# A second buffer for the exps computed on VectorE, one slot for Q's weights, and another plan of which exp blocks go there

## The chip, the cores and the metric

One NeuronCore of a Trainium2 chip runs the whole kernel. The metric is the device time of one execution in microseconds, as a median over runs.

## The reference

Two branches work on the same x (2048 tokens of 1024 features) and a sigmoid gate mixes them per token. A is a state-space model (SSM) with a complex diagonal recurrence, B is attention with 32 heads of 32 features.

```python
g = sigmoid((x * gate_w).sum(-1, keepdims=True))
# A
Lam_bar = exp(exp(log_dt) * Lam);  B_bar = ((Lam_bar - 1) / Lam)[:, None] * Bmat
h_t = Lam_bar * h_(t-1) + B_bar x_t            # complex, 1024 states
a = 2 * (h @ Cmat.T).real + x * Dskip
# B
q, k, v = split_heads(x @ wqkv)                # 32 heads of 32
b = softmax(q k^T * 32 ** -0.5) v  @ wo
out = g * a + (1 - g) * b
```

## The kernel before

**The loop.** Attention sets the order. It goes through 8 groups of 4 heads; a group has 8 units of 256 queries, and a unit 8 bursts of 256 keys. That makes 512 bursts, numbered 0 to 511; unit U holds bursts 8U to 8U+7. `burst` writes 8 score matmuls (L1615) to two of three PSUM slots and two exps of 128x1024 on ScalarE (L1634), one for each pair of heads. `pv` multiplies the results with V (L1700) some bursts later, and `normalize` (L1713, L1714) closes a unit.

**Exps shared with VectorE.** `X_PLAN` and `X_AT` choose bursts in pairs. In a chosen burst the second exp covers only 768 of its 1024 columns (L1631). For the other 256, VectorE reads the scores into a fixed-point tile `xi` (L1624, "the read"). The short exp on ScalarE also waits for this read, since its operation has it in `deps`. When both bursts of a pair have been read, `x_ops` gives three polynomial steps on VectorE (L1658, L1659, L1655) and one on GpSimd (L1656); `x_pv` then multiplies the result with V (L1679). `xi` holds one pair. So, ahead of a chosen burst, `build` runs whatever steps are still pending:

```python
            while p in self.x_of and self.xbg:
                self.x_flush()
            second = self.burst(p)
```

`X_AT` is ((0, 2), (4, 6)): an entry of `X_PLAN` that is a multiple of 8 takes bursts 0 and 2 of its unit, the other kind bursts 4 and 6. There are 92 entries, from 112 to 504, so 184 short exps.

**Everything else** is cut into dense chains of 8 or more matmuls, of which some four go into each burst: the projections to Q, K (`d_qk`, L1418) and V (`d_v`, L1436), the SSM's input chains u (`d_u`, L1448), its output chains c (`d_c`, L1495, L1501) and the output projection (`d_out`, L1526). Each chain ends in an evacuation of PSUM bank 7 on VectorE: L1425, L1442, L1452 (u), L1508 (c), L1538. Between those, VectorE does the work of the SSM: tables (L1328, L1331), folding factors into C (`fold_ops`, L1311 to L1313), and for each of 32 items (8 blocks of states by 4 stretches of time) elementwise steps (L1346) and scans (L1355).

**The planner.** `build` writes the order out when the program is made. It keeps a guess of VectorE's time (`dve_t`) with a cost for each step, and puts as many waiting steps into each burst as end in time for the next evacuation. Output chains of a stretch of time begin once its items are done and all of C is folded.

**Weights.** `wb` has two slots of Q, K and V weights (one for even groups, one for odd) and three of B. `ld_w` loads all three parts for the group after next at burst 25 of a group. Wo's rows later take the place of weights that have had their last use: `wo3` and `wo` name the places. All these DMAs are issued by SyncE (SP), whose queue runs in order.

Of the kernel before, what the change touches and what calls it, by code (L numbers as in the profile page):

```python
# [922 lines left out]
GROUPS = 8  # L923
QUNITS = 8
BURSTS = 8
NBURST = GROUPS * QUNITS * BURSTS
# [7 lines left out]

X_AT = ((0, 2), (4, 6))
X_PLAN = (112, 116, 120, 124, 128, 132, 136, 140, 144, 148, 152, 156, 160, 164, 168, 172, 176, 180, 184, 188, 192, 196, 200, 204, 208, 212, 216, 220, 224, 228, 232, 236, 240, 244, 248, 252, 256, 260, 264, 268, 272, 276, 280, 284, 288, 292, 296, 300, 304, 308, 312, 316, 328, 352, 356, 360, 364, 368, 372, 376, 380, 384, 388, 392, 396, 400, 404, 408, 412, 416, 420, 424, 428, 432, 436, 440, 444, 448, 452, 456, 460, 464, 468, 472, 476, 480, 484, 488, 492, 496, 500, 504)
X_COLS = 256
# [5 lines left out]
X_A = SCALE * math.log2(math.e) * 65536.0  # L943
X_LO = -127.0 * 65536.0
# [14 lines left out]
class FastPath:  # L959

    def __init__(self, nc, S, es, d, flag):
        self.nc, self.S, self.d, self.flag = nc, S, d, flag
        E = es.enter_context
        T = lambda name, shape, dt: E(nc.sbuf_tensor("f_" + name, shape, dt))
# [20 lines left out]
        self.hp = hp  # L985
        self.hpx = wb[:, 6144:9216].rearrange("p (k n) -> p k n", k=6)
# [71 lines left out]
    def ld_x(self, i, eng="sp"):  # L1058

        for r, n in ((0, 128), (1, 128)) if i == 0 else ((2 * i, 256),):  # L1060
            self.dma(lambda e, r=r, n=n: e.dma_start_transpose(self.xT[:, :, 128 * r:128 * r + n], self.x2[128 * r:128 * r + n, :]),  # L1061
                     [], [("xr", r + k) for k in range(n // 128)], "ld_x", eng)

    def ld_w(self, g, part, eng="sp"):
        cb = 1024 * part + 128 * g
        self.dma(lambda e: e.dma_start(self.w[:, g % 2, part], self.wsrc[:, :, cb:cb + 128]), [], [("w", g % 2, part)], "ld_w", eng)

# [54 lines left out]
    def piece(self, part, i, bank, first):  # L1122

        ps, w, xT = self.ps, self.w, self.xT
        for h in range(2):
            r = 2 * i + h

            def mm(e, r=r, h=h):
                m = None
                for a in range(8):  # L1130
                    m = e.matmul(ps[:, bank, 128 * h:128 * (h + 1)], w[:, 0, part, a, :], xT[:, a, 128 * r:128 * (r + 1)], start=(a == 0), stop=(a == 7))
                return m
            kw = dict(writes=[("bank", bank)]) if h == 0 else dict(acc=[("bank", bank)])
            yield lambda mm=mm, kw=kw, r=r: self.S.op("pe", mm, reads=[("w", 0, part), ("xr", r)], name="proj", **kw)

    def half256(self, part, i, half):
        ps, w, xT = self.ps, self.w, self.xT

        def mm(e):
            m = None  # L1140
            for a in range(4 * half, 4 * half + 4):
                m = e.matmul(ps[:, 7, 0:256], w[:, 0, part, a, :], xT[:, a, 256 * i:256 * (i + 1)], start=(a == 0), stop=(a == 7))
            return m
        self.S.op("pe", mm, reads=[("w", 0, part), ("xr", 2 * i), ("xr", 2 * i + 1)], name="proj", **(dict(acc=[("bank", 7)]) if half else dict(writes=[("bank", 7)])))

    def opening(self):
        S, ps, w, xT, dve = self.S, self.ps, self.w, self.xT, self.dve

# [8 lines left out]
        for word in self.OPENING.split():  # L1157
            op = word.rstrip("0123456789.")
            i = word[len(op):]
# [16 lines left out]
            elif op in ("Va", "Vb"):  # L1176
                bank, h, kt = 6, int(op == "Vb"), 2 * i + int(op == "Vb")
# [236 lines left out]
    def d_qk(self, g, part, ch, bank=7):  # L1414
        ps, w, xT = self.ps, self.w, self.xT
        mms = []
        for a in range(8):
            mms.append((1, lambda e, f, l, a=a: e.matmul(ps[:, bank, :], w[:, g % 2, part, a, :], xT[:, a, 512 * ch:512 * (ch + 1)], start=f, stop=l),  # L1418
                        [("w", g % 2, part)] + self.xtok(ch)))
        if part == 0:  # L1420
            z = (4 * g + ch) % 5
            dst, tok = self.Q[:, z, :], ("Q", z)
        else:
            dst, tok = self.K[:, g % 2, 512 * ch:512 * (ch + 1)], ("K", g % 2, ch)
        return self.chain(mms, "proj", lambda: self.dve(lambda e: e.tensor_copy(dst, ps[:, bank, :]), [("bank", bank)], [tok], "evac_qk"), bank)  # L1425

    def d_v(self, g, f, bank=7):
        ps, w, xT = self.ps, self.w, self.xT
        mms = []
        for q in range(4):  # L1430
            kt = 4 * f + q
            for half in range(2):
                def fn(e, first, last, q=q, kt=kt, half=half):
                    m = None
                    for a in range(4 * half, 4 * half + 4):
                        m = e.matmul(ps[:, bank, 128 * q:128 * (q + 1)], xT[:, a, 128 * kt:128 * (kt + 1)], w[:, g % 2, 2, a, :],  # L1436
                                     start=(a == 0), stop=(a == 7))
                    return m
                mms.append((1, fn, [("w", g % 2, 2)] + self.xtok(f)))
# [163 lines left out]
    def burst(self, B):  # L1603
# [17 lines left out]
        if mine is not None:  # L1621
            b, n = mine
            s = sl[1]
            first = self.dve(lambda e: e.tensor_scalar(self.xi[:, X_COLS * n:X_COLS * (n + 1)], ps[:, 2 * s + 1, 512 - X_COLS:512], X_A, X_LO, ALU.mult, ALU.max),  # L1624
                             [("S", s)], [("xi", n)], "x_in")
        def exp(z):
# [17 lines left out]
    def x_ops(self, b):  # L1644

        xi, xq, xp = self.xi, self.xq, self.xp
# [4 lines left out]
        i2, p2 = [("xi", 0), ("xi", 1)], [("xp", 0), ("xp", 1)]  # L1651

# [72 lines left out]
    def build(self):  # L1725
# [55 lines left out]
        for p in range(first, NBURST):  # L1781
# [40 lines left out]
            if pg == 25 and g + 2 < GROUPS:  # L1822
                assert g or not (proj[0] or cur and cur.tag == "proj")
                for part in (1, 2, 0):
                    self.ld_w(g + 2, part)
            wsv = self.d["B_wo"].rearrange("(a p) n -> p a n", p=128)
            if p == 386:
                self.dma(lambda e: e.dma_start(self.wo3[0], wsv[:, 0:3, :]), [], ["wo0"] + [("w", 0, q) for q in range(3)], "ld_wo")
            if not cs and cur is None and not wo1 and self.c_left[3] == 0:
                wo1 = True  # L1830
                self.dma(lambda e: e.dma_start(self.wo3[1], wsv[:, 3:6, :]), [], ["wo1"] + [("bT", r) for r in range(3)] + [("hp", 8, k) for k in range(6)], "ld_wo")
            if g >= 6 and not wo6 and not cs and self.c_left[3] == 0:
                wo6 = True
                self.dma(lambda e: e.dma_start(self.wo3[3], wsv[:, 6:7, :]), [], ["wo3", ("cT", 0, 0), ("cTf", 0, 0, 0), ("cTf", 0, 0, 1)], "ld_wo")
            if g >= 6 and not last and not proj[7] and not us and not cs and cur is None and not self.bg:

                last = True
                xs = [("xr", r) for r in range(16)]
                assert wo1 and wo6
                self.dma(lambda e: e.dma_start(self.wo3[2], wsv[:, 7:8, :]), [], ["wo2"] + [("w", 1, q) for q in range(3)] + xs, "ld_wo")  # L1840
            if g >= 6 and not cs and self.c_left[3] == 0 and nal < 8 and p > self.c_end:
# [280 lines left out]
```

## Time and profile before

| | |
|---|---|
| median of 3 runs | 931.43 us (930.91 to 931.58) |
| profiled execution, its own time | 928.48 us |
| its span, first to last instruction | 926.7 us |
| mean granted TensorE clock | 0.998 |
| ScalarE busy | 908.3 us, 1034 instructions |
| TensorE busy | 883.7 us, 15095 matmuls |
| VectorE busy | 758.9 us, 1310 instructions |
| GpSimd busy | 74.4 us, 156 instructions |

In the profile's rows PE is TensorE, PEld its weight loads, ACT ScalarE, DVE VectorE, POOL GpSimd and SPq SyncE's issue of DMAs. A row of the groups has line, engine, operation, out<-in and shapes with their count, then total busy us and mean ns of one, then the engine's idle us just before them and who ended it. A row of the timeline has start and length in us; a bracket at its end is the idle time before it and its releaser. Consecutive alike instructions are merged into one row (x3).

### The profile page before, as it was taken

Reading aid. Unit: us, or ns where it says so; the run is one execution under the profiler, and the core shown is the slowest. Engines: PE = TensorE matmul, PEld = TensorE weight load, DVE = VectorE, ACT = ScalarE, POOL = GpSimd, SP = SyncE. Lnnn points to the kernel's source line nnn. Section 1 sums busy time; section 2 is a strip of 40 time slices with the busy share of each in tenths; the row PEclk is TensorE's granted clock in tenths of the full one; section 3 lists DMA queues with packets and bytes.
Section 4 is the critical chain, followed back from the end, with each engine's and each line's share of the span. In section 5 each row is a group of like instructions: output and inputs, shape, how many; then the busy total and the mean of one; then the engine's idle time right before and its main releaser. Section 6 shows DMA issues by size and latency. Waiting matters only on the chain.

```text
span 926.7 us, 33866 instructions
## 1 busy us (share of the span) xinstructions
PE 883.7 (95%) x15095; PEld 502.8 (54%) x15316; DVE 758.9 (82%) x1310; ACT 908.3 (98%) x1034; POOL 74.4 (8%) x156
## 2 busy tenths in 40 slices
PE   8899999999999999999999999999999999989995
PEld 4555744447555565556655565555655655545553
DVE  2789989888989989889898989998998655676665
ACT  6999999999999999999999999999999999999997
POOL 2000000000100100102110100100010010001000
PEclk9999999999999999999999999999999999999999
DMA  9579737730114305572011511523002012424312
GB/s 205 93 127 167 115 80 137 156 86 16 42 53 102 70 20 102 120 160 52 19 51 53 122 38 27 120 64 102 19 17 65 21 48 74 145 85 123 118 63 75
DMA packets 170920, 77.71 MB, mean 84 GB/s; under 512 B 147216, under 2 KB 155408, under 8 KB 170768
## 3 DMA queue, kind: packets, MB, share of 16 engines
q1 hardware_dynamic: 168608, 74.94, 35.9%
q8 instruction: 121, 1.98, 0.9%
q10 hardware_dynamic: 2160, 0.53, 0.3%
q14 instruction: 31, 0.25, 0.1%
HBM read 25.18 MB, written 20.97 MB: 50 GB/s over the span
## 4 chain that ended last, share of the span: by engine, by line
PE 51%; ACT 36%; DVE 8%; issue 2%; DMA 1%; SPq 1%; DVEq 0%; ACTq 0%
ACT f_pt L1634 28%; PE f_ps L1700 11%; PE f_ps L1615 11%; PE f_ps L1495 8%; PE f_ps L1418 8%; PE f_ps L1448 6%; PE f_ps L1436 5%; ACT f_pt L1631 4%; DVE f_xi L1624 3%; ACT f_cT L1634 2%; ACT f_OT L1634 1%; ACT f_Et L1634 1%; SPq L1061 1%; PE f_ps L1679 1%; DMA f_xT<-in_A_x_dram 1%
## 5 line engine op out<-in xcount | busy, mean ns | idle before, releaser
L1634 ACT ACTIVATE f_pt<-f_ps 128x1024 bf16<-128x1024 f32 x760 | 727.7, 1113 | 1.2 <-PE f_ps L1615 1.0
L1700 PEld LDWEIGHTS f_ps<-f_V,f_pt 128*128 128x128 bf16 x7184 | 222.4, 96 | 94.8 <-issue 67.5
L1700 PE MATMUL f_ps<-f_V,f_pt 128*128 128x33 bf16 x7184 | 257.9, 178 | 0.3 <-ACT f_pt L1634 0.3
L1615 PE MATMUL f_ps<-f_Q,f_K 32*128 32x256 bf16 x4096 | 203.4, 273 | 14.4 <-ACT f_pt L1634 5.6
L1631 ACT ACTIVATE f_pt<-f_ps 128x768 bf16<-128x768 f32 x184 | 162.8, 885 | 3.0 <-DVE f_xi L1624 1.6
L1615 PEld LDWEIGHTS f_ps<-f_Q,f_K 32*128 32x128 bf16 x4096 | 60.8, 92 | 152.3 <-ACT f_pt L1634 125.4
L1448 PE MATMUL f_ps<-f_xT,f_wb 128*128 128x512 bf16 x448 | 117.7, 379 | 7.9 <-issue 2.3
L1418 PE MATMUL f_ps<-f_xT,f_wb 128*128 128x512 bf16 x406 | 106.7, 379 | 4.2 <-DVE f_K L1425 0.3
L1656 POOL TENSOR_SCALAR f_xp<-f_xq 128x512 int16<-128x512 f32 x92 | 57.3, 623 | 603.5 <-DVE f_xq L1655 385.9
L1624 DVE TENSOR_SCALAR f_xi<-f_ps 128x256 int32<-128x256 f32 x184 | 77.7, 423 | 19.5 <-PE f_ps L1615 13.7
L1355 DVE TENSOR_TENSOR_SCAN f_ht<-f_pf,f_init,f_ut 128x512 bf16<-128x512 f32 x64 | 79.7, 1272 | 0.0
L1495 PE MATMUL f_ps<-f_cT,f_hp 128*128 128x512 bf16 x240 | 67.6, 379 | 2.1
L1658 DVE SCALAR_TENSOR_TENSOR f_xq<-f_xi 128x512 f32<-128x512 uint16 x92 | 63.7, 692 | 3.1
L1659 DVE SCALAR_TENSOR_TENSOR f_xq<-f_xq,f_xi 128x512 f32<-128x512 f32 x92 | 63.6, 692 | 3.1
L1655 DVE SCALAR_TENSOR_TENSOR f_xq<-f_xi,f_xq 128x512 f32<-128x512 int16 x92 | 63.6, 691 | 2.7
L1448 PEld LDWEIGHTS f_ps<-f_xT,f_wb 128*128 128x128 bf16 x512 | 40.0, 96 | 40.6 <-issue 8.6
L1436 PE MATMUL f_ps<-f_wb,f_xT 128*128 128x128 bf16 x896 | 59.3, 219 | 0.0
L1526 PE MATMUL f_ps<-f_wb,f_OT 128*128 128x512 bf16 x186 | 55.0, 379 | 2.9 <-DVE f_Et L1538 0.9
L1418 PEld LDWEIGHTS f_ps<-f_xT,f_wb 128*128 128x128 bf16 x464 | 36.1, 96 | 35.4 <-issue 7.6
L1452 DVE CAST f_ub<-f_ps 128x512 bf16<-128x512 f32 x64 | 44.1, 689 | 11.8 <-PE f_ps L1448 9.2
L1436 PEld LDWEIGHTS f_ps<-f_wb,f_xT 128*128 128x128 bf16 x896 | 50.4, 97 | 3.8 <-issue 3.8
L1713 DVE RECIPROCAL f_rc<-f_ps 128x8 f32<-128x8 f32 x63 | 13.1, 207 | 44.2 <-PE f_ps L1679 35.7
(149 smaller groups left out, 797.7 us busy)
## 6 DMA issues: line engine op xcount, KB each, us to landing
u_scratch<-f_ub SPq DMA_DIRECT2D x64, 128.0 KB, 2.0
f_ub<-u_scratch SPq DMA_DIRECT2D x32, 256.0 KB, 2.8
ag_scratch<-f_Ag SPq DMA_DIRECT2D x32, 256.0 KB, 2.0
f_hp<-ag_scratch SPq DMA_DIRECT2D x32, 256.0 KB, 3.0
f_wb<-in_B_wqkv_dram SPq DMA_DIRECT2D x21, 256.0 KB, 4.2
out_dram<-f_xT SPq DMA_DIRECT2D x16, 256.0 KB, 2.0
f_wb<-in_B_wo_dram SPq DMA_DIRECT2D x2, 768.0 KB
f_OT<-f_On SPq DMA_TRANSPOSE x63, 2.3
```

What stands on the lines that cost most here:

```text
L1355: ops.append((1.24, lambda ri=ri: dve(lambda e: e.tensor_tensor_scan(ht[:, ri, :], rr, ut[:, ri, :], self.init[:, ri, j:j + 1], ALU.mult, ...
L1418: mms.append((1, lambda e, f, l, a=a: e.matmul(ps[:, bank, :], w[:, g % 2, part, a, :], xT[:, a, 512 * ch:512 * (ch + 1)], start=f, stop=l ...
L1436: m = e.matmul(ps[:, bank, 128 * q:128 * (q + 1)], xT[:, a, 128 * kt:128 * (kt + 1)], w[:, g % 2, 2, a, :], start=(a == 0), stop=(a == 7))
L1448: mms.append((1, lambda e, f, l, a=a: e.matmul(ps[:, 7, :], bT[:, (2 * n + ri) % 3, a, :], xT[:, a, 512 * ch:512 * (ch + 1)], start=f, sto ...
L1495: mms.append((1, lambda e, f, l, j=j, ri=ri, h=h: e.matmul(ps[:, 7, :], h[:, cols], cT[ri][:, j, 512 * cb:512 * (cb + 1)], start=f, stop=l ...
L1615: m = e.matmul(ps[:, 2 * sl[h // 2] + h % 2, 256 * kl:256 * (kl + 1)], K[32 * h:32 * h + 32, g % 2, 128 * kt:128 * (kt + 1)], Q[32 * h:32 ...
L1624: first = self.dve(lambda e: e.tensor_scalar(self.xi[:, X_COLS * n:X_COLS * (n + 1)], ps[:, 2 * s + 1, 512 - X_COLS:512], X_A, X_LO, ALU.m ...
L1631: self.S.op("act", lambda e: e.activation(flat(self.tile[p]), flat(ps[:, 2 * s:2 * s + 2, :]), ACT.Exp, scale=SCALE), reads=[("S", s)], wr ...
L1634: self.act(lambda e: e.activation(self.tile[p], ps[:, 2 * s:2 * s + 2, :], ACT.Exp, scale=SCALE), [("S", s)], [("pt", p)], "exp")
L1655: self.dve(lambda e: e.scalar_tensor_tensor(xq[:], hi, 128.0 / X_K, xq[:], ALU.mult, ALU.add), i2 + ["xq"], ["xq"], "x_q")
L1658: return [(0.73, 0.0, lambda: self.dve(lambda e: e.scalar_tensor_tensor(xq[:], lo, E2 / E3 * w, lo, ALU.add, ALU.mult), i2, ["xq"], "x_q") ...
L1700: m = e.matmul(ps[:, 6, o:o + 33], self.tile[p][:, h2, 256 * kl + 128 * qt:256 * kl + 128 * (qt + 1)], V[:, g % 2, 2 * i + kl, h, :], star ...
```

## The change

- `xi` becomes two tiles, used in turn by pair (`b % 2`). The steps pending ahead of a chosen burst are run only at the first burst of a pair, and only while more than three are pending.
- `X_AT` gets a third choice, (0, 4). A unit whose second entry is missing from `X_PLAN` takes bursts 0 and 4 for its one pair.
- `X_PLAN` still has 92 entries. New are 64, 72, 80, 88, 92, 96, 100, 104, 108, 320, 324, 332, 336 and 344; gone are 140, 148, 156, 164, 196, 204, 212, 220, 268, 276, 284, 292, 300 and 308.
- Q's weights have one slot for all groups, loaded for the next group at burst 28; K's and V's keep two, loaded at burst 25. `wb` shrinks by 1024 columns. Q's chains may not begin before burst 32 of a group.
- Wo's first load at burst 386 has two rows instead of three; the third row goes to a place in C's tile (`wo4`), with a DMA of its own when the output chains are done.

```diff
-X_AT = ((0, 2), (4, 6))
+X_AT = ((0, 2), (4, 6), (0, 4))
...
-        wb = T("wb", [128, 9216], BF)
-        self.w = wb[:, 0:6144].rearrange("p (s q a n) -> p s q a n", s=2, q=3, a=8)
-        self.bT = wb[:, 6144:9216].rearrange("p (s a n) -> p s a n", s=3, a=8)
+        wb = T("wb", [128, 8192], BF)
+        self.wq = wb[:, 0:1024].rearrange("p (a n) -> p a n", a=8)
+        self.wkv = wb[:, 1024:5120].rearrange("p (s q a n) -> p s q a n", s=2, q=2, a=8)
+        self.bT = wb[:, 5120:8192].rearrange("p (s a n) -> p s a n", s=3, a=8)
...
-        self.xi = T("xi", [128, 2 * X_COLS], I32)
+        self.xi = T("xi", [128, 2, 2 * X_COLS], I32)
...
+    def w_of(self, g, part):
+        return (self.wkv[:, g % 2, part - 1], ("w", g % 2, part)) if part else (self.wq, ("w", 0, 0))
...
-            first = self.dve(lambda e: e.tensor_scalar(self.xi[:, X_COLS * n:X_COLS * (n + 1)], ...
-                             [("S", s)], [("xi", n)], "x_in")
+            first = self.dve(lambda e: e.tensor_scalar(self.xi[:, b % 2, X_COLS * n:X_COLS * (n + 1)], ...
+                             [("S", s)], [("xi", b % 2, n)], "x_in")
...
-                proj[g][8 + c].after = 16 * c
+                proj[g][8 + c].after = max(16 * c, 32)
...
-                self.x_plan(p // 8, X_AT[p // 4 % 2])
-            while p in self.x_of and self.xbg:
+                one = p % 8 == 0 and p + 4 not in X_PLAN and p < NBURST - 8
+                self.x_plan(p // 8, X_AT[2 if one else p // 4 % 2])
+            while p in self.x_of and self.x_of[p][1] == 0 and len(self.xbg) > 3:
                 self.x_flush()
...
             if pg == 25 and g + 2 < GROUPS:
...
-                for part in (1, 2, 0):
+                for part in (1, 2):
                     self.ld_w(g + 2, part)
+            if pg == 28 and g + 1 < GROUPS:
...
+                self.ld_w(g + 1, 0)
...
-                self.dma(lambda e: e.dma_start(self.wo3[0], wsv[:, 0:3, :]), [], ["wo0"] + [("w", 0, q) for q in range(3)], "ld_wo")
+                self.dma(lambda e: e.dma_start(self.wo3[0], wsv[:, 0:2, :]), [], ["wo0"] + [("w", 0, q) for q in (1, 2)], "ld_wo")
...
+                self.dma(lambda e: e.dma_start(self.wo3[4], wsv[:, 2:3, :]), [], ["wo4", ("cT", 0, 1), ("cTf", 0, 1, 0), ("cTf", 0, 1, 1)], "ld_wo")
```

More of the change, by code (lines that the diff above doesn't have):

```diff
@@ L1122, in piece @@
     def piece(self, part, i, bank, first):
-        ps, w, xT = self.ps, self.w, self.xT
+        ps, xT = self.ps, self.xT
+        w = self.w_of(0, part)[0]
         for h in range(2):
@@ L1130, in mm @@
                 for a in range(8):
-                    m = e.matmul(ps[:, bank, 128 * h:128 * (h + 1)], w[:, 0, part, a, :], xT[:, a, 128 * r:128 * (r + 1)], start=(a == 0), stop=(a == 7))
+                    m = e.matmul(ps[:, bank, 128 * h:128 * (h + 1)], w[:, a, :], xT[:, a, 128 * r:128 * (r + 1)], start=(a == 0), stop=(a == 7))
                 return m
@@ L1136, in half256 @@
     def half256(self, part, i, half):
-        ps, w, xT = self.ps, self.w, self.xT
+        ps, xT = self.ps, self.xT
+        w = self.w_of(0, part)[0]
         def mm(e):
@@ L1141, in mm @@
             for a in range(4 * half, 4 * half + 4):
-                m = e.matmul(ps[:, 7, 0:256], w[:, 0, part, a, :], xT[:, a, 256 * i:256 * (i + 1)], start=(a == 0), stop=(a == 7))
+                m = e.matmul(ps[:, 7, 0:256], w[:, a, :], xT[:, a, 256 * i:256 * (i + 1)], start=(a == 0), stop=(a == 7))
             return m
@@ L1414, in d_qk @@
     def d_qk(self, g, part, ch, bank=7):
-        ps, w, xT = self.ps, self.w, self.xT
+        ps, xT = self.ps, self.xT
+        w, tok = self.w_of(g, part)
         mms = []
         for a in range(8):
-            mms.append((1, lambda e, f, l, a=a: e.matmul(ps[:, bank, :], w[:, g % 2, part, a, :], xT[:, a, 512 * ch:512 * (ch + 1)], start=f, stop=l),
-                        [("w", g % 2, part)] + self.xtok(ch)))
+            mms.append((1, lambda e, f, l, a=a, w=w: e.matmul(ps[:, bank, :], w[:, a, :], xT[:, a, 512 * ch:512 * (ch + 1)], start=f, stop=l),
+                        [tok] + self.xtok(ch)))
         if part == 0:
@@ L1427, in d_v @@
     def d_v(self, g, f, bank=7):
-        ps, w, xT = self.ps, self.w, self.xT
+        ps, xT = self.ps, self.xT
+        w, wtok = self.w_of(g, 2)
         mms = []
@@ L1823, in build @@
                 assert g or not (proj[0] or cur and cur.tag == "proj")
-                for part in (1, 2, 0):
+                for part in (1, 2):
                     self.ld_w(g + 2, part)
+            if pg == 28 and g + 1 < GROUPS:
+                assert not (cur and cur.tag == "proj")
+                self.ld_w(g + 1, 0)
             wsv = self.d["B_wo"].rearrange("(a p) n -> p a n", p=128)
             if p == 386:
-                self.dma(lambda e: e.dma_start(self.wo3[0], wsv[:, 0:3, :]), [], ["wo0"] + [("w", 0, q) for q in range(3)], "ld_wo")
+                self.dma(lambda e: e.dma_start(self.wo3[0], wsv[:, 0:2, :]), [], ["wo0"] + [("w", 0, q) for q in (1, 2)], "ld_wo")
             if not cs and cur is None and not wo1 and self.c_left[3] == 0:
@@ L1839, in build @@
                 assert wo1 and wo6
-                self.dma(lambda e: e.dma_start(self.wo3[2], wsv[:, 7:8, :]), [], ["wo2"] + [("w", 1, q) for q in range(3)] + xs, "ld_wo")
+                self.dma(lambda e: e.dma_start(self.wo3[2], wsv[:, 7:8, :]), [], ["wo2"] + [("w", 1, q) for q in (1, 2)] + xs, "ld_wo")
             if g >= 6 and not cs and self.c_left[3] == 0 and nal < 8 and p > self.c_end:
```

23 lines of the change are left out of this document (12 added, 11 removed).

## The prediction

> **What bounds the kernel now.** I read the page's engine totals and costliest groups first, then busy time by stages, then the timeline where stages that should be alike differ.
>
> ```profile
> span 926.7 us, 33866 instructions
> PE 883.7 (95%) x15095; PEld 502.8 (54%) x15316; DVE 758.9 (82%) x1310; ACT 908.3 (98%) x1034; POOL 74.4 (8%) x156
> L1634 ACT ACTIVATE f_pt<-f_ps 128x1024 bf16<-128x1024 f32 x760 | 727.7, 1113 | 1.2 <-PE f_ps L1615 1.0
> L1631 ACT ACTIVATE f_pt<-f_ps 128x768 bf16<-128x768 f32 x184 | 162.8, 885 | 3.0 <-DVE f_xi L1624 1.6
> L1624 DVE TENSOR_SCALAR f_xi<-f_ps 128x256 int32<-128x256 f32 x184 | 77.7, 423 | 19.5 <-PE f_ps L1615 13.7
> L1658 DVE SCALAR_TENSOR_TENSOR f_xq<-f_xi 128x512 f32<-128x512 uint16 x92 | 63.7, 692 | 3.1
> ```
>
> ScalarE is busy 908.3 of 926.7 us. It runs 1024 exps, two for each of 512 bursts: 840 full ones of 1024 columns (760 of them in the L1634 row) and 184 short ones of 768 (L1631), whose other 256 columns VectorE computes. The mean durations, 1.113 and 0.885 us, overlap their neighbours, so I take the cost of one from the distance between ends. This is the timeline about burst 328:
>
> ```profile
> 592.56 4.05 ACT L1634 ACTIVATE f_pt<-f_ps 128x1024 bf16<-128x1024 f32 x4
> 596.20 1.11 ACT L1631 ACTIVATE f_pt<-f_ps 128x768 bf16<-128x768 f32 x1
> 597.11 2.95 ACT L1634 ACTIVATE f_pt<-f_ps 128x1024 bf16<-128x1024 f32 x3
> 599.84 0.93 ACT L1631 ACTIVATE f_pt<-f_ps 128x768 bf16<-128x768 f32 x1
> ```
>
> The ends are 596.61, 597.31, 600.06 and 600.77. A short exp takes 0.70 us, three full ones 2.75, one 0.917; a shortened exp saves 0.21. All exps back to back are 840 x 0.917 + 184 x 0.70 = 899 us. ScalarE's 908.3 thus holds some 9 us of anything else, waits included. No change that keeps 184 short exps can gain more than about that. The next view, busy time by stages, shows where a part of it lies:
>
> ```profile
> core 0: us, PE busy (x) PEld busy (x) DVE busy (x) ACT busy (x) POOL busy (x), PEclk, DMA share, GB/s
> 129.10:216.90 87.80, 82.60 (x1374) 44.50 (x1393) 76.61 (x101) 87.80 (x97) 2.83 (x10) 1.00 0.56 117
> 244.80:301.80 57.00, 55.51 (x914) 30.32 (x929) 51.74 (x87) 56.01 (x65) 5.55 (x12) 1.00 0.28 78
> 301.80:357.10 55.30, 54.37 (x987) 32.78 (x996) 50.18 (x85) 55.30 (x66) 5.34 (x11) 1.00 0.22 44
> 468.20:525.60 57.40, 55.58 (x916) 30.39 (x931) 51.62 (x87) 56.05 (x66) 5.59 (x12) 1.00 0.28 78
> 525.60:580.80 55.20, 54.27 (x984) 32.69 (x993) 49.94 (x85) 55.20 (x65) 5.24 (x11) 1.00 0.20 45
> ```
>
> The last four are bursts 128 to 160, 160 to 192, 256 to 288 and 288 to 320: each 32 bursts with 48 full and 16 short exps, 48 x 0.917 + 16 x 0.70 = 55.2 us. The second and fourth take just that. The first and third hold the SSM's output chains and take 57.0 and 57.4: 1.7 and 2.2 us more than their neighbours, 3.9 in all. The timeline at burst 144 shows the loss, the one at burst 140 the same chain end without it:
>
> ```profile
> 272.28 1.96 ACT L1634 ACTIVATE f_pt<-f_ps 128x1024 bf16<-128x1024 f32 x2
> 272.65 0.73 DVE L1508 TENSOR_SCALAR f_Ag<-f_ps,f_gcol 128x512 f32<-128x512 f32 x1
> 273.29 0.68 DVE L1655 SCALAR_TENSOR_TENSOR f_xq<-f_xi,f_xq 128x512 f32<-128x512 int16 x1
> 274.08 0.42 DVE L1624 TENSOR_SCALAR f_xi<-f_ps 128x256 int32<-128x256 f32 x1
> 274.54 0.81 ACT L1631 ACTIVATE f_pt<-f_ps 128x768 bf16<-128x768 f32 x1 [0.30 <-DVE f_xi L1624]
> ```
>
> ```profile
> 264.44 2.88 ACT L1634 ACTIVATE f_pt<-f_ps 128x1024 bf16<-128x1024 f32 x3
> 265.45 0.75 DVE L1508 TENSOR_SCALAR f_Ag<-f_ps,f_gcol 128x512 f32<-128x512 f32 x1
> 266.19 0.42 DVE L1624 TENSOR_SCALAR f_xi<-f_ps 128x256 int32<-128x256 f32 x1
> 267.17 0.85 ACT L1631 ACTIVATE f_pt<-f_ps 128x768 bf16<-128x768 f32 x1
> ```
>
> At 144, VectorE evacuates the chain (L1508), then runs the last polynomial step of the batch before (L1655), and only then reads the scores (L1624). The short exp waits for that. It ends at 275.35, 1.11 us after the exp before it (274.24): 0.40 over 0.70. At 140 nothing stands between L1508 and L1624. L1624 ends at 266.61, 0.56 before the exp starts, and the exp ends 0.70 after the one before it. Before the change, one xi tile forces this: all pending steps are flushed ahead of the next read. In its built order the sequence L1508, L1655, L1624 occurs 12 times, at bursts 132, 136, 144, 148, 152, 156 and 128 later: the two slow stages.
>
> **The change part by part.** *Second xi tile, and no flush of three or fewer pending steps.* In the changed kernel's built order, L1655 never stands between an output evacuation and a read of the scores, and each of the 24 evacuations that come directly ahead of a read stands as at burst 140. So the 3.9 us go, 0.33 for each of 12 places. As bounds, the idle row of L1631 gives DVE only 1.6 us, the least that can go; but it misses what overlapping durations hide (0.30 is named at burst 144, 0.40 was lost), so I take the stages. From them I leave 0.3 in, since the output chains also carry more TensorE work (55.5 against 54.4 us): 3.6.
>
> *Pairs moved.* There are 184 short exps before and after: 28 leave bursts 138 to 166, 194 to 222 and 266 to 310 (every fourth from 138, so the units there keep two), and 28 come to bursts 64 to 110 and 320 to 348. Each move loses 0.21 and gains 0.21: zero. VectorE, though, gets 18 reads and nine batches of three steps in bursts 64 to 112: 18 x 0.423 + 27 x 0.69 = 26.2 us on top of 76.6, in a stage of 87.8 that shrinks by 18 x 0.21 to 84.0. That doesn't fit, so the order puts off SSM items and the folding of C. The first eight items end at burst 117 instead of 94, folding at 157 instead of 116, and the first output chains begin at 158 instead of 124. The backlog is gone at burst 401 in both kernels and the last output chain ends at 433 in both, so it costs nothing at the end. TensorE needs 82.6 of those 84.0 us, 98.3%; the smooth stage has 54.37 of 55.30, also 98.3%.
>
> The new company of short exps is folding. In the built order ten reads have a fold step two places ahead, with one evacuation between; before it was one. The nearest rows without short exps:
>
> ```profile
> 138.64 1.28 DVE L1312 SCALAR_TENSOR_TENSOR f_cT<-f_cT,f_pf,f_OT 128x1024 bf16<-128x1024 bf16 x1
> 139.84 0.69 DVE L1452 CAST f_ub<-f_ps 128x512 bf16<-128x512 f32 x1
> 140.89 0.81 PE L1448 MATMUL f_ps<-f_xT,f_wb 128*128 128x512 bf16 x3 [0.56 <-DVE f_ub L1452]
> 138.99 4.11 ACT L1634 ACTIVATE f_pt<-f_ps 128x1024 bf16<-128x1024 f32 x4
> ```
>
> The fold step holds back the evacuation and TensorE idles 0.56 us, yet ScalarE's four exps run through. For ten places the ends are 0 (as here) and 10 x 0.40 = 4.0 us (as at burst 144). I take 0.5: an evacuation in 0.69 ends close to its due time, and the L1655 case had two VectorE steps back to back after the chain's end.
>
> GpSimd's step, too, falls beside folds. Rows of before:
>
> ```profile
> 252.72 0.62 POOL L1656 TENSOR_SCALAR f_xp<-f_xq 128x512 int16<-128x512 f32 x1 [7.52 <-DVE f_xq L1655]
> 253.08 0.79 DVE L1346 TENSOR_TENSOR f_ut<-f_ht,f_tq 128x512 f32<-128x512 bf16 x1
> L1346 DVE TENSOR_TENSOR f_ut<-f_ht,f_tq 128x512 f32<-128x512 bf16 x64 | 43.6, 697 | 0.9
> ```
>
> Two SBUF inputs beside GpSimd's read, and L1346 takes 0.79 for a mean of 0.70; 0.1 is lost, well inside the 0.56 of slack at burst 140, so I book nothing. The Trainium skill, "SBUF — State Buffer", section "Who interferes with whom", says that of a VectorE instruction with two SBUF inputs and a GpSimd instruction that reads SBUF, the later one blocks fully until the first ends. By that a fold step, or the GpSimd step, would wait its partner out; with a whole 0.62 against 0.56 of slack in nine batches the sum would be 0.5 us worse. The trace doesn't show a full block here: L1346 would have ended 0.70 after GpSimd's 253.34, at 254.04, and ended at 253.87.
>
> *A place left.* Burst 222 is short now and full afterwards:
>
> ```profile
> 408.83 0.69 DVE L1452 CAST f_ub<-f_ps 128x512 bf16<-128x512 f32 x1 [0.71 <-DMA u_scratch<-f_ub]
> 409.88 0.81 ACT L1631 ACTIVATE f_pt<-f_ps 128x768 bf16<-128x768 f32 x1
> 411.12 1.02 ACT L1634 ACTIVATE f_pt<-f_ps 128x1024 bf16<-128x1024 f32 x1 [0.42 <-PE f_ps L1615]
> ```
>
> A late store held the evacuation and then TensorE; the next exp ends 1.45 after the short one (410.69 to 412.14), 0.53 lost. As this is one late store, it can come again under any of the new short bursts that run beside u chains: from 0.5 gained to 0.5 lost, booked at zero.
>
> *One slot for Q's weights.* The load moves from burst 25 of a group to burst 28, its first use stands at burst 52 or later, and no reader of the slot is then outstanding. On SyncE's queue it only moves past three bursts of stores. What hides it is 24 bursts of over 1.6 us; without that cover only TensorE's spare work would wait.
>
> *Wo.* One of three rows loaded at burst 386 moves to burst 434 and takes an issue of its own ahead of the partial-sum loads:
>
> ```profile
> 784.25 0.49 SPq L1834 DMA_DIRECT2D f_cT<-in_B_wo_dram  x1
> f_wb<-in_B_wqkv_dram SPq DMA_DIRECT2D x21, 256.0 KB, 4.2
> 799.58 0.81 PE L1526 MATMUL f_ps<-f_wb,f_OT 128*128 128x512 bf16 x3
> ```
>
> One more issue of 0.49 and a landing like 4.2 us for 256 KB end near 790; the first output projection starts at 799.58. Zero, for 9 us of cover; without it, the wait would be on the path.
>
> **Sum.** -3.6 + 0.5 = -3.1 us, on the profiled execution's own 928.48 us: 925.4, a span of 923.6. The median of the runs shown, 931.43, lies 2.95 above that execution; the same ratio (0.9967) makes it 928.3.
>
> **The rivals.**
> *Folds hold up the reads* (slower). A fold step of 1.28 us ahead of an evacuation makes that late, and so the read and the short exp, as L1655 of 0.68 does now. It decides from 3.6 / 10 = 0.36 us for each of the ten places. At 0.55, if a longer step in front costs more than the 0.40 of burst 144, the result is 5.5 - 3.6 = +1.9: 933.3. For it speaks TensorE's 0.56 us of idle at 140; against it, ScalarE's unbroken row there.
>
> *TensorE is the floor of the slow stages.* They then fall only until it is busy 98.3%: 55.51 / 0.983 = 56.5 from 57.0, and 56.5 from 57.4: a gain of 1.4, 930.0. Its larger work in these stages speaks for it; against it, each unit there now has two short exps instead of four, so ScalarE needs longer for the same work.
>
> *The stalls only move.* The delayed last step comes due at its values' matmul, and the wait reappears there or under the new short bursts: 931.4. The built order has the last step at least one burst ahead of that matmul everywhere, which speaks against it.
>
> **How the numbers follow.** The forecast has 0.74, the fold rival 0.11, TensorE's floor 0.08, moved stalls 0.07. The forecast's own range: everything goes right (-3.9 - 0.5 - 0.4 of small events, 926.6) to folds at half their upper bound (+2.0 - 3.6, 929.8). Beyond that I leave out the fold rival and part of the moved stalls: 926.2 to 930.6. A measurement here tells 0.2% from no change, 1.9 us. Faster takes most of the forecast and a little of TensorE's floor, 0.76; same, the rest of those two and half of the moved stalls, 0.13; slower, 0.11.
>
> **What the profile after would show.** Right: the idle of L1631's group put down to the read of the scores falls from 1.6 us to near nothing; stages of 32 bursts with output chains take their exps' 0.917 and 0.70 and no more; 184 short exps at 0.70 between ends, also in bursts 64 to 110. Wrong: short exps of 1.0 or more between ends beside folds (bursts 119 to 157), TensorE over 98.5% busy with ScalarE's idle put down to L1615, or waits of the values' matmul for GpSimd.

## Result and profile after

| | median us | lowest to highest | executions |
|---|---|---|---|
| before, beside it on the same chip | 932.96 | 930.91 to 937.66 | 15 |
| after | 930.3 | 926.21 to 933.28 | 15 |

The ratio is 0.9961, 95% interval 0.9944 to 0.9978: 0.39% faster, where the prediction had 0.9967. The medians are 2.66 us apart, and 930.3 us stands where the prediction had 928.3. The profiled execution of after took 928.11 us, before's had taken 928.48: this pair differs by only 0.37 us, where the prediction had 3.1. First the page's totals and the groups by line and shape (busy us, mean ns | idle us ahead and what ended it):

```profile
span 926.3 us, 33979 instructions
PE 902.5 (97%) x15316; PEld 503.9 (54%) x15316; DVE 758.4 (82%) x1310; ACT 907.3 (98%) x1034; POOL 86.8 (9%) x156
L1643 ACT ACTIVATE f_pt<-f_ps 128x1024 bf16<-128x1024 f32 x760 | 728.8, 1090 | 1.5 <-PE f_ps L1624 1.3
L1640 ACT ACTIVATE f_pt<-f_ps 128x768 bf16<-128x768 f32 x184 | 165.3, 898 | 0.7 <-PE f_ps L1624 0.6
L1665 POOL TENSOR_SCALAR f_xp<-f_xq 128x512 int16<-128x512 f32 x92 | 67.3, 732 | 646.0 <-DVE f_xq L1664 471.3 <-PE f_ps L1688 161.3 <-PE f_ps L1624 7.2
```

The short exps (before's L1631, now L1640) no longer wait for VectorE's read: before's 1.6 us for it are gone from the row, and what is left names TensorE. But GpSimd's step L1665 (before's L1656) takes 0.732 us in the mean; before it was

```profile
L1656 POOL TENSOR_SCALAR f_xp<-f_xq 128x512 int16<-128x512 f32 x92 | 57.3, 623 | 603.5 <-DVE f_xq L1655 385.9 <-PE f_ps L1679 187.2 <-PE f_ps L1495 16.1
```

The stages of after, columns as in the prediction's view. The rows are bursts 64 to 112, 128 to 160, 160 to 192, 256 to 288 and 288 to 320:

```profile
131.20:215.60 84.40, 83.62 (x1398) 44.66 (x1396) 76.68 (x123) 84.30 (x98) 8.06 (x12) 1.00 0.63 122
243.30:299.80 56.50, 55.80 (x902) 28.54 (x899) 50.26 (x70) 56.50 (x65) 4.56 (x6) 1.00 0.64 132
299.80:355.50 55.70, 55.58 (x1006) 33.26 (x1003) 51.34 (x86) 55.70 (x65) 6.68 (x10) 1.00 0.12 33
468.20:525.50 57.30, 56.86 (x936) 30.67 (x933) 52.64 (x87) 56.96 (x66) 7.35 (x10) 1.00 0.31 82
525.50:582.00 56.50, 55.72 (x993) 32.63 (x990) 52.11 (x87) 56.50 (x65) 7.69 (x13) 1.00 0.22 54
```

With the exps that each now holds (0.917 us a full one, 0.703 a short one) the floors are 84.2, 56.5, 55.7, 56.5 and 56.5 us. Four rows are within 0.2 of their floor; the one of bursts 256 to 288 is 0.8 above.

To compare kernels finer than by stages, I use one number below, the **loss**: for each exp the distance from the end of the one before it to its own end, less 0.917 or 0.703, summed. From burst 16 on it is 8.48 us in before and 6.72 in after.

| loss, us | bursts 128–160 | 256–288 | 35–36 | 94–96 | 222–223 | from burst 16 |
|---|---|---|---|---|---|---|
| before, first profile | 1.75 | 2.11 | 0.18 | 0 | 0.54 | 8.48 |
| before, second (g2_before) | 1.76 | 2.10 | 0.88 | 0.08 | 1.00 | 9.87 |
| after, first profile | −0.02 | 0.72 | 1.44 | 0 | 0.44 | 6.72 |
| after, second (f4_after) | −0.01 | 0.73 | 4.23 | 3.15 | 0.16 | 12.51 |
| e1_oldplan | 1.79 | 1.80 | 4.02 | 0 | 0 | 11.83 |
| e2_plan | 0.68 | 0.73 | 2.98 | 2.23 | 1.12 | 12.72 |
| e3_q25 | −0.01 | 0.70 | 0.24 | 0 | 0 | 4.97 |
| e4_qslot | 1.74 | 2.10 | 1.14 | 0 | 0.28 | 9.09 |
| f1_old_gap | 2.07 | 2.07 | 3.41 | 0 | 0.11 | 11.81 |
| f2_q25_gap | −0.01 | 0.86 | 0.86 | 0 | 0 | 5.78 |
| f3_qslot25 | 1.76 | 2.12 | 0.37 | 0 | 0.89 | 9.35 |
| g1_old_gap3 | 1.05 | 1.06 | 0.14 | 0 | 0 | 6.15 |
| g3_before_w40 | 1.75 | 2.10 | 0.40 | 0 | 0 | 8.04 |
| g4_after_w40 | −0.01 | 0.73 | 0.52 | 0 | 0 | 5.36 |

The first two columns, the output chains, come out the same to 0.03 us in all five profiles with before's tile and plan, and in all four with after's that add nothing to VectorE. The next three differ by up to 3.15 us between two executions of one kernel (after's): a profile pair is not a measurement of them. What lies outside the exps from burst 16 (the first 16 bursts, 39.6 to 40.8 us, and what follows the last exp, 8.2 to 9.6) varies too; in the first pair it took back 1.3 of the 1.76 us.

### The profile page after: what moved, and what is told of

It reads as the page before. It is cut to its first block, busy times and chain, and to the rows that moved or that the text cites. A ratio compares the mean times of both kernels' runs of the same rounds, so it can differ in the third digit from the quotient of the medians.

```text
span 926.3 us, 33979 instructions
## 1 busy us (share of the span) xinstructions
PE 902.5 (97%) x15316; PEld 503.9 (54%) x15316; DVE 758.4 (82%) x1310; ACT 907.3 (98%) x1034; POOL 86.8 (9%) x156
## 4 chain that ended last, share of the span: by engine, by line
PE 52%; ACT 40%; DVE 4%; DMA 2%; SPq 1%; issue 1%; POOL 0%; DVEq 0%; ACTq 0%
ACT f_pt L1643 32%; PE f_ps L1709 14%; PE f_ps L1624 10%; PE f_ps L1426 9%; PE f_ps L1504 7%; PE f_ps L1457 6%; ACT f_pt L1640 5%; PE f_ps L1445 5%; SPq L1062 1%; ACT f_cT L1643 1%; PE f_ps L1688 1%; DMA f_xT<-in_A_x_dram 1%; ACT f_Et L1643 1%; DMA f_wb<-in_A_B_im_dram 1%; DMA f_ub<-u_scratch 0%
## 5 line engine op out<-in xcount | busy, mean ns | idle before, releaser
L1640 ACT ACTIVATE f_pt<-f_ps 128x768 bf16<-128x768 f32 x184 | 165.3, 898 | 0.7 <-PE f_ps L1624 0.6
L1457 PE MATMUL f_ps<-f_xT,f_wb 128*128 128x512 bf16 x512 | 131.5, 379 | 1.6 <-DMA f_wb<-in_A_B_im_dram 0.7
L1665 POOL TENSOR_SCALAR f_xp<-f_xq 128x512 int16<-128x512 f32 x92 | 67.3, 732 | 646.0 <-DVE f_xq L1664 471.3
L1426 PE MATMUL f_ps<-f_xT,f_wb 128*128 128x512 bf16 x464 | 119.3, 379 | 0.1
L1633 DVE TENSOR_SCALAR f_xi<-f_ps 128x256 int32<-128x256 f32 x184 | 77.4, 421 | 17.6 <-PE f_ps L1624 13.3
L1504 PE MATMUL f_ps<-f_cT,f_hp 128*128 128x512 bf16 x272 | 74.5, 379 | 0.1
L1664 DVE SCALAR_TENSOR_TENSOR f_xq<-f_xi,f_xq 128x512 f32<-128x512 int16 x92 | 63.5, 690 | 2.6
L1535 PE MATMUL f_ps<-f_wb,f_OT 128*128 128x512 bf16 x188 | 61.2, 381 | 0.4 <-DVE f_Et L1547 0.4
```

The costliest lines, as they stand in the source:

```text
L1426: mms.append((1, lambda e, f, l, a=a, w=w: e.matmul(ps[:, bank, :], w[:, a, :], xT[:, a, 512 * ch:512 * (ch + 1)], start=f, stop=l), [tok] ...
L1457: mms.append((1, lambda e, f, l, a=a: e.matmul(ps[:, 7, :], bT[:, (2 * n + ri) % 3, a, :], xT[:, a, 512 * ch:512 * (ch + 1)], start=f, sto ...
L1504: mms.append((1, lambda e, f, l, j=j, ri=ri, h=h: e.matmul(ps[:, 7, :], h[:, cols], cT[ri][:, j, 512 * cb:512 * (cb + 1)], start=f, stop=l ...
L1633: first = self.dve(lambda e: e.tensor_scalar(self.xi[:, b % 2, X_COLS * n:X_COLS * (n + 1)], ps[:, 2 * s + 1, 512 - X_COLS:512], X_A, X_LO ...
L1640: self.S.op("act", lambda e: e.activation(flat(self.tile[p]), flat(ps[:, 2 * s:2 * s + 2, :]), ACT.Exp, scale=SCALE), reads=[("S", s)], wr ...
L1665: self.pool(lambda e: e.tensor_scalar(bits, xq[:], X_K, 128.0 * (E0 + 126.0), ALU.mult, ALU.add), ["xq"], p2, "x_p")
```

## Experiments

Ratios are to before on the same chip, with 95% intervals.

**The tile without the plan: e1_oldplan.** After, with before's list of pairs. (The new third choice in `X_AT` also moves one short exp, from burst 330 to 332; the same holds for e4, f1, f3 and g1.)

```diff
-X_PLAN = (64, 72, 80, 88, 92, 96, 100, 104,
+X_PLAN = (112, 116, 120, 124, 128, 132, 136, 140,
...
```

> The changed kernel with X_PLAN of before: two xi tiles and no flush, but both pairs stay in the output chains. Theory (the flush ahead of the read made the 12 waits, the second tile takes them away): the stages of bursts 128 to 160 and 256 to 288 take 55.2 to 56 us for before's 57.0 and 57.4, ScalarE's idle put down to the read of the scores is below 0.2 us, and the ratio to before is 0.995 to 0.998. Rival (the gain comes from taking pairs out of the output chains): the two stages stay at 57 and the ratio is 0.999 to 1.002.

0.9974 (0.9953 to 0.9994). The short exps wait no more (the L1640 row has the same 0.7 us of idle as after's, and their loss is 0.88 us where before's is 4.5), yet the two output stages still lose 1.79 and 1.80, where before lost 1.75 and 2.11. The loss now sits on full exps: 0.26 and 0.29 at bursts 138 and 139, 0.28 and 0.29 at 154 and 155, the same 128 later. The timeline of e1 at burst 138:

```profile
263.23 0.73 DVE L1517 TENSOR_SCALAR f_Ag<-f_ps,f_gcol 128x512 f32<-128x512 f32 x1
263.88 0.41 DVE L1633 TENSOR_SCALAR f_xi<-f_ps 128x256 int32<-128x256 f32 x1
264.21 0.68 DVE L1664 SCALAR_TENSOR_TENSOR f_xq<-f_xi,f_xq 128x512 f32<-128x512 int16 x1
264.81 0.69 DVE L1353 TENSOR_TENSOR f_tq<-f_ht,f_Et 128x1024 bf16<-128x1024 bf16 x1
264.97 0.99 POOL L1665 TENSOR_SCALAR f_xp<-f_xq 128x512 int16<-128x512 f32 x1 [1.41 <-DVE f_xq L1664]
266.02 0.27 PE L1688 MATMUL f_ps<-f_V,f_xp 128*128 128x33 bf16 x4 [0.27 <-POOL f_xp L1665]
```

The read L1633 now precedes the last step L1664, as intended. But GpSimd's step L1665 then coincides with L1353, a VectorE step with two SBUF inputs, and takes 0.99 instead of 0.62. The values' matmul L1688 waits 0.27 for it, and behind L1688 on TensorE stand the next scores. The stall moved by a burst or two; this is the third rival, by a mechanism that it did not name. The small gain in time is not the tile's either: e1 also has Q's slot, and on the same chip its median is 931.31 us, that of the slot without the tile (e4, below) 931.15.

**The plan without the tile: e2_plan.** Before, with the new list, the rule for single pairs and the third choice of places; one xi tile and the full flush stay.

```diff
-X_AT = ((0, 2), (4, 6))
+X_AT = ((0, 2), (4, 6), (0, 4))
...
-                self.x_plan(p // 8, X_AT[p // 4 % 2])
+                one = p % 8 == 0 and p + 4 not in X_PLAN and p < NBURST - 8
+                self.x_plan(p // 8, X_AT[2 if one else p // 4 % 2])
```

> Before with the new X_PLAN and the choice (0, 4) alone: one xi tile, all pending steps flushed, Q's weights as before. Its built order has five flushes behind an evacuation (bursts 120, 256, 264, 336, 360) for before's 12. Theory: each of the five costs 0.2 to 0.55 us between ends of exps, the seven others are gone: 1.5 to 2.5 us gained, ratio 0.997 to 0.9985. Rival (the plan is what pays): as fast as the whole change, 0.996, with no wait for the read at the five places.

0.9992 (0.9973 to 1.0011): no gain is measured, though the interval still allows 2.5 us of one. Its short exps' row, before's being quoted in the prediction, has half the wait for the read:

```profile
L1631 ACT ACTIVATE f_pt<-f_ps 128x768 bf16<-128x768 f32 x184 | 164.5, 894 | 1.8 <-DVE f_xi L1624 0.8 <-PE f_ps L1615 0.6
```

Five places still flush ahead of the read (bursts 120, 256, 264, 336 and 360: 0.25, 0.34, 0.40, 0.34 and 0.25 us, 1.58 in all). At burst 264 the last step L1655 delays the read, and the short exp waits:

```profile
487.73 0.68 DVE L1655 SCALAR_TENSOR_TENSOR f_xq<-f_xi,f_xq 128x512 f32<-128x512 int16 x1
488.97 0.81 ACT L1631 ACTIVATE f_pt<-f_ps 128x768 bf16<-128x768 f32 x1 [0.29 <-DVE f_xi L1624]
```

Its 0.68 in bursts 128 to 160 is one wait at burst 159, behind a late store of u. Apart from that, e2 loses no more in the output stages than after does (0.73 against 0.72 in bursts 256 to 288). So the moved pairs, not the tile, take the 3.16 us from the output stages. The plan alone pays for this with 0.84 us at bursts 120, 336 and 360 and with the flushes at 256 and 264. The tile takes all five of these stalls away and leaves one of another kind in after, at burst 257:

```profile
468.47 0.68 DVE L1664 SCALAR_TENSOR_TENSOR f_xq<-f_xi,f_xq 128x512 f32<-128x512 int16 x1
469.07 0.68 DVE L1353 TENSOR_TENSOR f_tq<-f_ht,f_Et 128x1024 bf16<-128x1024 bf16 x1
469.23 0.99 POOL L1665 TENSOR_SCALAR f_xp<-f_xq 128x512 int16<-128x512 f32 x1 [1.41 <-DVE f_xq L1664]
470.29 0.27 PE L1688 MATMUL f_ps<-f_V,f_xp 128*128 128x33 bf16 x4 [0.27 <-POOL f_xp L1665]
471.86 1.02 ACT L1643 ACTIVATE f_pt<-f_ps 128x1024 bf16<-128x1024 f32 x1 [0.16 <-PE f_ps L1624]
```

It costs 0.26 and 0.29 where the first exps of bursts 258 and 259 end. Under the new plan the tile is thus worth some 1.0 us in the profiles (1.58 less 0.55).

**The GpSimd step by itself: f1_old_gap, f2_q25_gap, g1_old_gap3.** A VectorE memset of unused columns, which reads nothing, is put behind L1664 where its values' matmul is due next: six places under the old plan (f1, on e1 with Q's load as in e3), three under the new (f2, on e3). g1 is f1 with three memsets.

```diff
+            due = [q for q, bs in self.x_when.items() if b in bs][0]
+            if self.p + 1 >= due and self.p < 320:
+                for _ in range(3):
+                    self.dve(lambda e: e.memset(self.rc[:, 41:63, :], 0.0), [], [("rc", u) for u in range(41, 63)], "gap")
```

> The kernel with two tiles and X_PLAN of before, group 1's Q weights at burst 25, and a VectorE memset of 22x8 elements (no SBUF input, about 0.25 us) right behind the last polynomial step wherever the values' matmul is due in the next burst: bursts 136, 144, 152, 264, 272 and 280. Theory (there the GpSimd step L1665 waits behind a VectorE step with two SBUF inputs, takes 1.0 us for 0.62, and TensorE waits for it): the GpSimd step starts beside the memset and takes 0.62, TensorE's idle put down to GpSimd falls from 1.1 us to about 0, and the output-chain stages of bursts 128 to 160 and 256 to 288 lose under 0.5 us each for 1.8. Rival (the steps simply come too late behind the evacuation, whatever GpSimd does): with 0.25 us more on VectorE these stages lose as much or more.

> The changed kernel with group 1's Q weights at burst 25 and the same memset (bursts 120, 256, 264). Theory: the wait of 0.55 us at burst 258 goes, otherwise as with the load at 25 alone; ratio to before 0.993 to 0.996, and 1.5 to 2 us under the change. Rival: the wait at 258 stays.

> As with one memset behind the last polynomial step at bursts 136, 144, 152, 264, 272 and 280, but with three of them (about 0.5 us in all). With one, the next VectorE step with two SBUF inputs still began 0.02 us after the GpSimd step's recorded start, and the GpSimd step ended 0.47 us after that VectorE step's end, as without a memset. Theory (GpSimd's step is held for the whole of a VectorE step with two SBUF inputs): with 0.5 us between, the GpSimd step takes 0.62 to 0.7 at these places, TensorE's idle put down to GpSimd goes from 1.6 us to under 0.3, and the stages of bursts 128 to 160 and 256 to 288 lose 1 us or less each for 2.07. Rival (the last step comes too late in any case): TensorE's idle and the losses stay or grow.

f1 0.9981 (0.9963 to 0.9999), f2 0.9945 (0.9928 to 0.9962). One memset did not free GpSimd, and in both kernels the stall stayed; f1 at burst 138:

```profile
263.49 0.68 DVE L1664 SCALAR_TENSOR_TENSOR f_xq<-f_xi,f_xq 128x512 f32<-128x512 int16 x1
264.16 0.20 DVE L1668 MEMSET f_rc<- 128x176 f32 x1
264.26 1.12 POOL L1665 TENSOR_SCALAR f_xp<-f_xq 128x512 int16<-128x512 f32 x1 [1.40 <-DVE f_xq L1664]
264.28 0.63 DVE L1353 TENSOR_TENSOR f_tq<-f_ht,f_Et 128x1024 bf16<-128x1024 bf16 x1
```

GpSimd's record begins before L1353's, and it still ends 0.47 us after it (265.38 against 264.91), as in e1 (265.96 against 265.50). The stall grows by the delay instead (0.39 for 0.26 at burst 138, and in f2 at burst 258). With three memsets, 0.82 us, the two no longer meet; g1 at burst 138:

```profile
259.51 0.68 DVE L1664 SCALAR_TENSOR_TENSOR f_xq<-f_xi,f_xq 128x512 f32<-128x512 int16 x1
260.18 0.82 DVE L1669 MEMSET f_rc<- 128x176 f32 x3
260.28 0.62 POOL L1665 TENSOR_SCALAR f_xp<-f_xq 128x512 int16<-128x512 f32 x1 [1.40 <-DVE f_xq L1664]
260.92 0.63 DVE L1353 TENSOR_TENSOR f_tq<-f_ht,f_Et 128x1024 bf16<-128x1024 bf16 x1
```

GpSimd takes 0.62, the values' matmul waits for nothing, and the losses at bursts 138 and 154 (and 128 later) are gone. The output stages lose 1.05 and 1.06 instead of 1.79 and 1.80, with VectorE given more to do, not less. That settles the mechanism of these stalls: it is the meeting of GpSimd with a VectorE step that has two SBUF inputs, not VectorE's load. In after, too, 18 of the 92 GpSimd steps take 0.99 us or more, each behind such a VectorE step, which it outlasts by 0.41 to 0.48 us; the other 74 take 0.62. TensorE waits for only one of the 18. What g1 still loses at bursts 139, 147 and 155 (0.14, 0.17 and 0.19) has no cause shown.

The other order, with GpSimd's step first, can be read in before:

```profile
315.73 0.62 POOL L1656 TENSOR_SCALAR f_xp<-f_xq 128x512 int16<-128x512 f32 x1 [7.15 <-PE f_ps L1700]
315.91 0.97 DVE L1346 TENSOR_TENSOR f_ut<-f_ht,f_tq 128x512 f32<-128x512 bf16 x1
```

VectorE's step ends 0.53 us after GpSimd's (316.88 against 316.35). The prediction's pair at 252.72 and 253.08 has the same 0.53 (253.87 against 253.34), although VectorE's step began 0.18 us later beside GpSimd's and took only 0.79. In these rows whichever comes second ends at a fixed distance behind the first: GpSimd's step at 0.46 to 0.47 us, L1346 at 0.53, each 0.15 to 0.17 less than it takes alone (0.62 and 0.70). g1 has one execution (926.51 us), so its time alone tells little.

**Q's slot and its load: e4_qslot, e3_q25, f3_qslot25.** e4 has only the one slot (with its load at burst 28 of a group) and Wo's place; tile, flush and the list of pairs are before's. e3 is after with group 0's Q load put back to burst 25; f3 is e4 with the same.

```diff
-            if pg == 28 and g + 1 < GROUPS:
+            if pg == (25 if g == 0 else 28) and g + 1 < GROUPS:
```

> Q's single slot and Wo's new place alone: before's X_PLAN, one xi tile, the full flush. Theory (Q's weights for group 1, loaded at burst 28, hold up the load of u that the first item waits for): the 12 waits as before, and VectorE waits 2 to 2.5 us for f_ub at about 70 us for before's 1.1, with some 1.3 us of ScalarE idle behind it: 1.3 us slower than before, ratio 1.001 to 1.002. Rival (that wait was an accident of one execution): no such wait, ratio 1.000.

> The changed kernel with group 1's Q weights loaded at burst 25, with K's and V's, instead of 28; the other groups at 28. Theory: VectorE's wait for f_ub at about 71 us falls from 2.4 us to 1.1 or less and ScalarE's idle of 1.34 us at burst 36 goes: 1.3 us faster than the change, ratio to before 0.994 to 0.996. Rival (accident, or the transfer itself and not its place delays the load of u): no difference from the change, the wait stays.

> Q's single slot and Wo's new place on before's plan with one tile and the full flush, but group 1's Q weights at burst 25. Theory (the place of that load costs 1 us): VectorE's wait for f_ub at 70 us is 1.1 to 1.3 us for the 2.1 with the load at 28, and burst 35 loses 0.2 for 1.1; ratio to before 0.998 to 1.001. Rival (the single slot itself changes the time): ratio under 0.997 or over 1.002.

e4 0.9982 (0.9967 to 0.9997), e3 0.9946 (0.9925 to 0.9967), f3 0.9964 (0.9945 to 0.9982). Two expectations missed here: e4 was to be 1.3 us slower than before and f3 at most 0.2% faster; e4 is 0.18% faster and f3 0.36%. Group 0 shows what the later load displaces. SyncE's queue and the step behind it in before, then in after:

```profile
66.14 1.30 SPq L1076 DMA_TRANSPOSE f_cT<-in_A_C_im_dram  x1
67.55 1.16 SPq L1465 DMA_DIRECT2D f_ub<-u_scratch  x1
71.41 0.69 DVE L1346 TENSOR_TENSOR f_ht<-f_ub,f_Et 128x1024 bf16<-128x1024 bf16 x1 [1.12 <-DMA f_ub<-u_scratch]
```

```profile
66.79 1.30 SPq L1081 DMA_TRANSPOSE f_cT<-in_A_C_im_dram  x1
68.14 1.28 SPq L1071 DMA_DIRECT2D f_wb<-in_B_wqkv_dram  x1
69.53 0.67 SPq L1474 DMA_DIRECT2D f_ub<-u_scratch  x1
73.34 0.69 DVE L1353 TENSOR_TENSOR f_ht<-f_ub,f_Et 128x1024 bf16<-128x1024 bf16 x1 [2.39 <-DMA f_ub<-u_scratch]
75.27 0.57 PE L1709 MATMUL f_ps<-f_V,f_OT 128*128 128x33 bf16 x16 [1.24 <-DVE f_On L1723]
77.36 1.02 ACT L1643 ACTIVATE f_OT<-f_ps 128x1024 bf16<-128x1024 f32 x1 [1.34 <-PE f_ps L1624]
```

The 256 KB load stands directly ahead of the first load of u. VectorE waits 2.39 us for that instead of 1.12, the normalization queued behind it (L1723) is late, TensorE waits 1.24 and ScalarE 1.34. With the load at burst 28 the wait was 2.4, 2.3, 2.2 and 2.1 us (after, f4, e1, e4); in the other ten profiles it was 1.0 to 1.8. In e3 it is 1.19 and the loss at bursts 35–36 is 0.24 instead of 1.44 and 4.23. That loss is not this wait's alone, though: f1, with the load at 25 as well, lost 3.41 there, and e2, with before's loads, 2.98. The intervals of e3 and after, and of f3 and e4, overlap, so by time the load's place is not shown to matter.

**Scatter, and loads at burst 40: f4_after, g2_before, g3_before_w40, g4_after_w40.** The first two are the kernels unchanged, profiled again. g3 and g4 are before and after with each weight load of a group at burst 40.

```diff
-            if pg == 25 and g + 2 < GROUPS:
+            if pg == 40 and g + 2 < GROUPS:
...
-            if pg == 28 and g + 1 < GROUPS:
+            if pg == 40 and g + 1 < GROUPS:
```

> The changed kernel as it is, for a second profile and for times beside the others. Theory: the wait for f_ub at 71 us is 2.0 to 2.5 us again with over 1 us lost at burst 35, the wait for GpSimd at burst 258 (0.55) is there again, no short exp waits for the read; ratio 0.995 to 0.998. Rival (these waits were accidents): either is missing.

> The kernel before, for a second profile. Its first profiled execution, 928.48 us, is shorter than every one of its timed runs. Theory (the executions differ by waits for DMAs of the u chains some bursts after the weight loads at burst 25 of a group, that is about bursts 35, 95, 159 and 223): there is 1 us or more of such losses beyond the first profile's 0.5 at 35 and 223, and the rest (12 waits for the read, 0.20 to 0.55) is as before to 0.05 us. Rival (they differ in the opening or everywhere): the losses at these bursts are as in the first profile.

> Before with the weights of the group after next loaded at burst 40 of a group, when no u chain runs, instead of 25. Theory (Q's single slot helps because it takes a load out of the bunch that the u chains' DMAs then stand behind): losses at bursts 35, 95, 159 and 223 are under 0.3 us each, times scatter less, ratio to before 0.995 to 0.998. Rival (the gain of Q's single slot with the old plan, 0.9964, is from another thing): ratio 0.999 to 1.001.

> The changed kernel with all weight loads, Q's too, at burst 40 of a group. Theory: no losses at bursts 35, 95 and 223, the wait at 258 (0.55) stays, no short exp waits for the read; 1 to 4 us under the change, ratio to before 0.991 to 0.9945. Rival (loads at burst 40 only move the waits, to the projections or to the loads of C): ratio as with the change, 0.9956 to 0.9961, with new losses behind burst 40.

f4 0.9956 (0.9931 to 0.998), g3 0.9959 (0.9944 to 0.9975), g4 0.9939 (0.992 to 0.9957). The second profile of after took 934.57 us against 928.11, and the table puts 5.9 of that at bursts 35–36 and 94–96. Its waits (engine, what for: sum us, count, longest):

```profile
PEld f_ps L1457 <- DMA f_wb<-in_A_B_im_dram: 4.3, 3, 2.1
DVE f_ht L1353 <- DMA f_ub<-u_scratch: 2.3, 1, 2.3
```

TensorE waits for the SSM's B, 6 to 10 bursts after the weight loads. With the weights at burst 40 (g4) PEld's row is gone, and of these waits there are left

```profile
DVE f_ht L1353 <- DMA f_ub<-u_scratch: 1.5, 1, 1.5
PE f_ps L1457 <- DMA f_wb<-in_A_B_im_dram: 0.2, 1, 0.2
```

and bursts 94–96 and 222–223 lose nothing in either kernel's profile. But nor do they in e1, e3, f2 and g1 (0.00 us), whose K and V loads stand at burst 25, so this alone shows no gain from the move. Before at burst 40 gains 0.41% by time without any other edit; that is clear of noise. g4 has the lowest ratio of all, but its interval overlaps after's, e3's and f2's. Against g3, which has the weights at the same place, it is 2.7 us faster by median (927.01 for 929.73) and by loss (5.36 for 8.04).

## Why the prediction was right, and where it was not

As a ratio the forecast was off by 0.06% (0.9967 for 0.9961). That is partly luck: of the sum's terms only some stood, and a part booked at zero made up for what was missing.

- *Flush, −3.6.* The stall was read rightly and the read is never late in after; the output stages gave 3.16 (3.86 to 0.70). But the sum gave all of it to the tile and the shorter flush. With them and the old pairs the output stages still lost 3.59 (e1). The sum also left 0.3 us in, for the wrong reason (TensorE's work).
- *Pairs moved, 0.* The exps do cancel, but the places do not: with one tile and the full flush the new pairs alone leave 0.73 us in the output stages apart from the late store, and 0.84 at three new places (e2).
- *Both together, by time.* f2 has everything of the new kernel except the late Q load, and three memsets; f3 has the Q slot without tile and plan. They ran on the same chip at 927.2 and 929.27 us, a difference of 2.1, where their profiles differ by 3.6 of loss. g4 and g3 differ by 2.7.
- *The third rival, 0.07.* "The built order has the last step at least one burst ahead of that matmul everywhere" failed as a reason. One burst isn't enough when GpSimd's step between them is held. It is just what the second tile alone does (e1), and the moved pairs avoid it at all places but one. That one, at burst 257, is also one of the prediction's signs of being wrong: a wait of the values' matmul for GpSimd.
- *GpSimd beside VectorE, 0.* This step was wrong. I read no full block from L1346 at 253.08, because it ended sooner than 0.70 us after GpSimd; but 0.53 behind GpSimd's end is what a full block looks like there, as the later row with 0.97 shows. And I looked at no row in which GpSimd came second: there it ended 0.46 to 0.47 us after VectorE in three kernels. The Trainium skill, "SBUF — State Buffer", section "Who interferes with whom", says that the later of the two blocks fully until the first is done; e1 and g1 agree (0.99 with the meeting, 0.62 without). After pays 0.55 us for it at burst 257; under the old plan the output stages lost 3.59 with it (e1), 2.11 without (g1, its memsets included).
- *Folds, +0.5.* Measured 0.01: bursts 114 to 158, which hold them, lose that much in after. The fold rival (0.11) falls, and so does TensorE's floor (0.08): bursts 128 to 160 reached their exps' floor with TensorE busy 55.80 of 56.50 us, 98.8%, bursts 160 to 192 with 99.8%.
- *Q's slot, 0.* "On SyncE's queue it only moves past three bursts of stores" was wrong. In group 0 a load of u stands next on that queue: by the traces about 1 us more of wait there. By time the slot gained instead: with Wo's new place, but without tile and plan, it made 0.9982, and 0.9964 with group 0's load at burst 25.
- *Burst 222, 0.* 0.44 was lost there, but from 0 to 1.12 in the others: scatter, as the booking assumed.

So the forecast's total was nearly right while its parts were not: some 2 us of the gain came from tile and plan together, and the rest, by e4's ratio, from the slot that was booked at zero; with intervals of some 1.5 us to either side this division is rough. No run parts the slot from Wo's new place. What stays open is how the slot gains. Before issues three weight loads together at burst 25 of a group. f3 parts one from the others (except in group 0), g3 moves all three, and both time at 0.996 although their profiles show no such gain over before's (losses 9.35 and 8.04 against 8.48 and 9.87). Before's medians beside the experiments, 933 to 934, lie some 3 to 5.5 us above its two profiled executions. It would fit all of this if the bunch of loads delays many executions, but neither of the two profiled; no trace shows it.

## What to carry to other kernels

When an in-order engine is relieved of a step at one place, ask where the step goes next: which engine waits for its result, and which instruction that engine's step will then meet. Judge interference from a row in which the instruction you care about came second, and by how far its end lies behind the other's end rather than by how long it took. When a DMA is moved, read the queue at the new place to the next load that somebody waits for. Before you credit one part of a change, build each part without the other: here the tile was credited with what the moved pairs did. Profile a kernel twice before a difference under 1% is put down to a stall beside DMAs.

## Unexpected on the chip

- GpSimd's 0.62 us step ends 0.47 us after a VectorE step with two SBUF inputs, whether its record begins 0.16 us after VectorE's (0.99 long) or 0.02 before it (1.12 long): here a record's start does not tell which of the two was held. A gap of 0.20 us ahead of the VectorE step was too short, 0.82 was enough.
- A 256 KB load ahead of another on SyncE's queue lengthened the wait for the second by about 1 us, and the losses some 6 to 10 bursts after weight loads differed between two executions of one kernel (after) by 2.8 us at one place (1.44 and 4.23) and 3.15 at another (0 and 3.15).
